# A longer pause, other tile counts and another order of small steps in the side work of an FNet + H3 kernel

## The chip, the cores and the metric

The kernel runs on one core of one Trainium2 chip. The metric is the device time of one execution in microseconds (us), the median of several runs. TensorE is called PE here (its weight loads PEld), VectorE DVE, ScalarE ACT, GpSimd POOL and SyncE SP. SP, ACT and POOL also issue transfers; SPq, ACTq and POOLq mark such an issue.

## What is computed

Four layers on x of 2048 x 576 floats: an FNet layer A, an H3 layer B, and both again with the same weights.

```python
def reference(A_x, A_dft_seq_re, A_dft_seq_im, A_dft_hid_re, A_dft_hid_im, B_q, B_k, B_v, B_shift_k, B_ssm_k, B_ssm_D):
    def _A_ref(x, dft_seq_re, dft_seq_im, dft_hid_re, dft_hid_im):
        a = jnp.einsum("bsd,ed->bse", x, dft_hid_re)
        b = jnp.einsum("bsd,ed->bse", x, dft_hid_im)
        return jnp.einsum("ts,bse->bte", dft_seq_re, a) - jnp.einsum("ts,bse->bte", dft_seq_im, b)
    def _B_ref(q, k, v, shift_k, ssm_k, ssm_D):
        # k_shift: causal convolution of k over 4 rows
        kv = k_shift * v
        # y: causal convolution of kv with ssm_k over all 2048 rows, by FFT of length 4096
        y = y + kv * ssm_D[None, None, :]
        return q * y
    x = A_x
    x = x + _A_ref(_layernorm(x, axis=-1), ...)
    x = x + _B_ref(_layernorm(x, axis=-1), B_k, B_v, ...)
    x = x + _A_ref(_layernorm(x, axis=-1), ...)
    x = x + _B_ref(_layernorm(x, axis=-1), B_k, B_v, ...)
    return x
```

In B only q is the running x. The long convolution of k_shift * v with ssm_k depends on inputs alone, so its result y can be made once, beside the first A, and used by both B layers.

## The kernel before, in words

**Number format.** Every float32 operand of a matmul is split into a rounded part (hi, made by ACT) and a remainder (lo, made by DVE, which subtracts hi), and a product is three matmuls: hi by hi, hi by lo, lo by hi. A split is thus an ACT instruction and then a DVE instruction.

**Main work.** The first A runs in steps n = 0 to 127 (function `layer`): four blocks of rows by real and imaginary part by 16 pieces of the sum. A step has 12 matmuls of 512 columns into four accumulators (`s`) and 2 into a fifth (`rm`). It is handed over in two parts, after 6 matmuls and at its end; at each hand-over the outer loop may put side work in. The constants of a step are loaded by SP (`flts<-in_c_mat`, 256 KB) and split by ACT and DVE (L93, L94) two steps ahead, into three tiles. When a block ends, its second product, over the hidden dimension, is left as eight pieces of 27 matmuls of 288 columns ("hidden pieces", `bk<-w,u`; DVE adds each result on L291). They are put in at odd steps and in the middle of the next block.

**Side work.** The generator `branch` makes y. Its first stage is over before step 47. Then come the two stages that the change edits:

- The **middle stage** has 37 pieces n. Each has a kernel half (`mid_kernel`: three matmuls; ACT evicts the result in three instructions into two `kk` tiles), a signal half (`mid_signal`: three matmuls; DVE multiplies and adds in four instructions, L565 to L568) and, two pieces later, an inverse (`mid_inverse`: three matmuls; ACT evicts into `vo`, ACT's queue issues the store to `vd` in DRAM, L589 and L591). Between the signal half and the inverse, `mid_round` splits the product into the one tile `yf`. `split_mid(n)` splits the input of piece n, and `load_mid(n)` loads it: even ones in one transfer into a `land` tile, odd ones in two, into the `apart` tiles.
- The **inverse stage** has 16 rows j, each in two halves (`i2_products`: six matmuls of 288 columns on `mid`; ACT evicts into a `vo` tile, ACT's queue stores that to `yb`, L650). A row is loaded from `vd` into a `land` tile (`load_row`, SP, 576 KB) and split (`split_row`); its constants come on POOL's queue (`load_fc`). A row load reads what every piece of the middle stage stored, so the first one waits for the last store.

**Order.** All of ACT's side-work instructions go through `act` (L505), which chains each behind the one before in the program's order; `act_split` does the DVE part on L510. Loads go through `load_after` (L167), on SP. SP, ACT, DVE and PE each work through their queues in order; the program's scheduler may put independent work of different stages in another order than the loop does. Three PSUM banks (`bk`) are shared by hidden pieces, the middle stage and the inverse stage.

**Pace.** The outer loop counts main work in `passed` and side work in `spent`. Each `yield` of `branch` names a cost, and at each hand-over up to `GROUPS` = 2 pieces are taken while side work lags:

```python
total = (I2_END + 1 - MID_FROM) * STEP + 3 * 2 * TB * PIECE
work = 37 * sum(MID_COST) + 2 * MID_PAUSE + 32 * I2_COST
...
for _ in range(0 if near else GROUPS):
    if spent < work * min(1.0, passed / total):
        with behind(*added, *evac):
            spent += next(br, work)
```

`total` is 65 x 3.2 + 24 x 3.6 = 294.4 and `work` is 37 x 7.3 + 8 + 32 x 1.9 = 338.9. A pause is a `yield` with a cost and no work.

Of the kernel before, what the change touches and what calls it, by code (L numbers as in the profile page):

```python
# [17 lines left out]
D = 576  # L18
J = S // P
TB = 4  # L20
NT = 512
HD = D // 2
# [19 lines left out]
MW = 504  # L42
MID_COST = (2.9, 2.6, 1.8)
MID_PAUSE = 4.0
BORDER = {J - 1: 0.5, 0: 0.75}
I2_COST = 1.9
GROUPS = 2
# [14 lines left out]
RT_AT = SC_AT + 4 * REM + 5 * WIDE  # L62
# [4 lines left out]
def fnet_h3_kernel(ctx: ExitStack, tc: tile.TileContext, x, c_mat, w_re, w_im, k_pad, v, shift_k,  # L67
# [44 lines left out]
    def flat(words, dt, name):  # L112
        return sb.tile([P, words], dt, tag=name, name=name)
# [17 lines left out]
    def lay(t, at, *sizes):  # L131

        for name, words, n in sizes:
            ring.setdefault(name, Ring()).tiles.extend(t[:, at + i * words:at + (i + 1) * words] for i in range(n))
            at += n * words
        assert at <= t.shape[1], (at, t.shape, sizes)
        return at
# [5 lines left out]
    def two(v):  # L143
        return v.rearrange("p (a n) -> p a n", a=2)
# [11 lines left out]
    flts = flat(FLT, F32, "flts")  # L156
# [8 lines left out]
    def load_after(dst, src):  # L165
        with tc.issue_after(anchor[-1]):
            return nc.sync.dma_start(dst, src).ins  # L167
# [186 lines left out]
    def branch():  # L354
# [148 lines left out]
        def act(*args, **kw):  # L503
            with behind(*last_act[-1:]):
                last_act.append(nc.scalar.activation(*args, **kw).ins)  # L505

        def act_split(h, l, src):
            act(h, src, AF.Copy)
            with behind(*products[-1:]):
                nc.vector.tensor_tensor(l, src, h.bitcast(F32), OP.subtract)  # L510
# [6 lines left out]
        def width(n):  # L517
            first, count = mids[n]
            return MW if n < groups else count * RW

        def load_mid(n):
            if n < len(mids):
                first, count = mids[n]
                w = width(n)
                landed[n] = [r[:, :w] for r in apart] if n % 2 else [ring["land"]()[:, :2 * w]]
                ends = landed[n] if n % 2 else [two(landed[n][0])[:, i] for i in range(2)]
                src = t_d[4 * first:4 * (first + count)]
                if n < groups:
                    src = src.rearrange("q j c s d -> (q j c) s d")[:, :, :MW]
                    if n % 2:  # L530
                        for i in range(2):
                            load_after(ends[i], src[:, i])
                    else:
                        load_after(two(landed[n][0]), src)
                else:
                    src = src.rearrange("(g q) j c s d -> (q j c) s g d", q=4)
                    for i in range(2):
                        load_after(ends[i].rearrange("p (g d) -> p g d", g=count), src[:, i, :, MW:])

        def split_mid(n):  # L540
            if n < len(mids):
                df, at = ring["df"](), 0
                halves[n] = df[:, :2 * width(n)], df[:, 2 * MW:2 * MW + 2 * width(n)]
                for src in landed.pop(n):
                    cs = slice(at, at + src.shape[1])
                    act_split(halves[n][0][:, cs], halves[n][1][:, cs], src)
                    at = cs.stop

        def mid_half(df, o, w):
            ps = bank()  # L550
            mm(ps[:, :w], mc[:, 0, :], df[0][:, o:o + w], True, False)
            mm(ps[:, :w], mc[:, 0, :], df[1][:, o:o + w], False, False)
            mm(ps[:, :w], mc[:, 1, :], df[0][:, o:o + w], False, True)
            return ps[:, :w]

        def mid_kernel(df, w):
            pk, p1, p2 = mid_half(df, w, w), ring["kk"]()[:, :w], ring["kk"]()[:, :w]
            act(p1[lo], pk[lo], AF.Copy)
            act(p1[hi], pk[lo], AF.Copy)
            act(p2[hi], pk[hi], AF.Copy)  # L560
            return p1, p2

        def mid_signal(df, w, p1, p2):
            px = mid_half(df, 0, w)
            nc.vector.tensor_tensor(p1, px, p1, OP.mult)  # L565
            nc.vector.scalar_tensor_tensor(p2[lo], px[hi], -1.0, p2[hi], op0=OP.mult, op1=OP.mult)
            nc.vector.tensor_tensor(p2[hi], px[lo], p2[hi], OP.mult)
            products.append(nc.vector.tensor_tensor(p1, p1, p2, OP.add).ins)  # L568
            return p1

        def mid_round(p1):
            w = p1.shape[1]
            yf = ring["yf"]()
            yf = yf[:, :w], yf[:, w:2 * w]
            act_split(*yf, p1)
            return yf

        def mid_inverse(n, yf):
            w = width(n)
            pv = bank()  # L580
            mm(pv[:, :w], mc[:, 2, :], yf[0], True, False)
            mm(pv[:, :w], mc[:, 2, :], yf[1], False, False)
            mm(pv[:, :w], mc[:, 3, :], yf[0], False, True)
            vo = ring["vo"]()[:, :w]
            act(vo, pv[:, :w], AF.Copy)
            first, count = mids[n]
            dst = v_d[4 * first:4 * (first + count)]
            if n < groups:
                nc.scalar.dma_start(dst.rearrange("q j c d -> (q j c) d")[:, :MW], vo)  # L589
            else:  # L590
                nc.scalar.dma_start(dst.rearrange("(g q) j c d -> (q j c) g d", q=4)[:, :, MW:],  # L591
                                    vo.rearrange("p (g d) -> p g d", g=count))
# [2 lines left out]
        for n in range(2):  # L595
            load_mid(n)
        yield 0
        for n in range(2):
            split_mid(n)
            load_mid(n + 2)  # L600
        for n in range(len(mids)):
            if n > 1:
                mid_inverse(n - 2, yf)
                yield MID_COST[2]
            df, w = halves.pop(n), width(n)
            kk = mid_kernel(df, w)
            if n:
                yf = mid_round(product)
            yield MID_COST[0]
            product = mid_signal(df, w, *kk)  # L610
            split_mid(n + 2)
            load_mid(n + 4)
            yield MID_COST[1]
# [4 lines left out]
        mid_inverse(n, yf)  # L618
        fresh("land", "vo", "df")
        lay(m1, 0, ("df", 4 * D, 2), ("fc", 4 * P, 3))  # L620
        assert lay(flts, 8 + NT, ("land", 2 * D, 3), ("vo", HD, 2)) <= RT_AT - 3 * HD

        def load_row(j):
            if j < J:
                landed[j] = ring["land"]()
                load_after(landed[j], v_d[:, j].rearrange("p c d -> p (c d)"))

        def load_fc(j):
            if j < J:
                fcs[j] = quads(ring["fc"]())  # L630
                load_fr(fcs[j], i2c[j])

        def split_row(j):
            if j < J:
                halves[j] = parts2(ring["df"]())
                act_split(*halves[j], landed.pop(j))
# [4 lines left out]
        def i2_products(hf, j, fc, vf):  # L641
            yo = ring["vo"]()
            ps = bank()
            for c in range(2):
                cs = slice(c * D + hf * HD, c * D + (hf + 1) * HD)
                mm(ps[:, :HD], fc[:, c, :], vf[0][:, cs], c == 0, False)
                mm(ps[:, :HD], fc[:, c, :], vf[1][:, cs], False, False)
                mm(ps[:, :HD], fc[:, 2 + c, :], vf[0][:, cs], False, c == 1)
            act(yo, ps[:, :HD], AF.Copy)
            nc.scalar.dma_start(yb_d[j][:, hf * HD:(hf + 1) * HD], yo)  # L650

        for j in range(3):
            load_fc(j)
        yield MID_PAUSE
        for j in range(3):
            load_row(j)
        yield MID_PAUSE
        for j in range(2):
            split_row(j)
            load_row(j + 3)  # L660
        for j in range(J):
            vf, fc = halves.pop(j), fcs.pop(j)
            i2_products(0, j, fc, vf)
            yield I2_COST
            i2_products(1, j, fc, vf)
            load_fc(j + 3)
            split_row(j + 2)
            load_row(j + 5)
            yield I2_COST

    def sums(src, junk):
# [119 lines left out]
    next(br)  # L791
    spent = passed = 0.0
    total = (I2_END + 1 - MID_FROM) * STEP + 3 * 2 * TB * PIECE
    work = 37 * sum(MID_COST) + 2 * MID_PAUSE + 32 * I2_COST
    for n, whole in layer(get_x0, lambda j: x[:, j, :], done0, pending):
        if (whole or whole is not None and n % J < J - 1) and n <= F1_END:
            at = n if whole else n - 0.5
# [12 lines left out]
        if n >= MID_FROM:  # L810
            if whole is not None:
                passed += STEP * (4 if whole else 3) / 7 * BORDER.get(n % J, 1.05)
            if whole is None or whole and n % 2 == 1 and n % (2 * J) < J - 1 and pending:
# [350 lines left out]
```

## Time and profile before

| | us |
|---|---|
| median of three runs | 1201.93 |
| the three runs | 1203.1, 1197.94, 1201.93 |
| the profiled execution, whole | 1201.85 |
| its span, first to last instruction | 1199.8 |
| PE busy in the span | 1177.4 |
| middle stage, first to last matmul, about | 215 to 530 |
| inverse stage, first to last matmul, about | 541 to 622 |

The page's rows name a line, an engine, an operation and a tile: `ACT L505 ... flts<-bk` is an eviction of a bank by ACT, `mid<-flts` on the same line the rounded part of a split. In brackets behind a row of the timeline stands how long the engine had been idle and what ended that. In a row of windows there follow the busy time of PE, PEld, DVE, ACT and POOL (instructions in parentheses), the granted PE clock as a share of full speed, the busy share of the core's 16 DMA engines, and GB/s. In the waits view the numbers are the total in us, the times, and the longest.

### The profile page before, as it was taken

What the parts mean: (1) busy time and instruction counts of PE and PEld (TensorE: products, weight loads), DVE (VectorE), ACT (ScalarE), POOL (GpSimd) and SP (SyncE); (2) the same over time, 40 slices, a digit from 0 to 9 for tenths busy, and PEclk for the clock granted to TensorE, in tenths of its full rate; (3) what the DMA queues carried; (4) which work ended last, traced back from release to release, by engine and by line L of the source; (5) the groups of instructions that cost most, each with busy time, mean ns of one, the idle gap of its engine ahead of it and who ended that gap; (6) DMA issues with size and microseconds to landing.
All of it is one profiled execution on the core that took longest, in us unless ns stands there. A gap on an engine that the chain in (4) does not pass through costs nothing.

```text
span 1199.8 us, 17259 instructions
## 1 busy us (share of the span) xinstructions
PE 1177.4 (98%) x6077; PEld 1012.8 (84%) x6077; DVE 813.8 (68%) x1335; ACT 615.3 (51%) x1106; POOL 65.8 (5%) x100
## 2 busy tenths in 40 slices
PE   7999999999999999998999999999999999999997
PEld 6888888888888877787888898888888888889997
DVE  7899794677766677643337766774775776874674
ACT  7965665567665566634445667544444445540110
POOL 2200000000000000001001111000000000001111
PEclk9999999999999999999999999999999999999999
DMA  9889897555575546458948687872493497696631
GB/s 356 277 263 321 258 302 240 181 166 174 170 253 182 170 130 171 110 150 271 284 149 281 230 252 235 276 252 88 147 330 93 135 332 269 191 345 191 202 122 40
DMA packets 153768, 257.69 MB, mean 215 GB/s; under 512 B 27601, under 2 KB 68817, under 8 KB 153682
## 3 DMA queue, kind: packets, MB, share of 16 engines
q1 hardware_dynamic: 113074, 205.58, 53.6%
q10 hardware_dynamic: 36000, 42.63, 10.2%
q0 software_dynamic: 4608, 8.39, 2.6%
q8 instruction: 47, 0.77, 0.3%
q14 instruction: 39, 0.32, 0.1%
HBM read 189.89 MB, written 66.65 MB: 214 GB/s over the span
## 4 chain that ended last, share of the span: by engine, by line
PE 89%; DMA 6%; DVE 2%; ACT 1%; issue 1%; SPq 0%; POOLq 0%; POOL 0%; DVEq 0%; ACTq 0%
PE s L76 51%; PE bk L76 33%; PE rm L76 5%; DMA yb<-flts 4%; DMA flts<-in_c_mat 1%; ACT flts L505 1%; DMA vd<-flts 0%; DMA flts<-t 0%; ACT mid L505 0%; DMA flts<-vd 0%; DVE flts L182 0%; DVE u L94 0%; DVE mats L94 0%; DVE mid L510 0%; ACT mats L196 0%
## 5 line engine op out<-in xcount | busy, mean ns | idle before, releaser
L76 PE MATMUL s<-mats 128*128 128x512 f32 x2088 | 524.6, 392 | 0.0
L76 PEld LDWEIGHTS s<-mats 128*128 128x128 f32 x2088 | 386.0, 188 | 80.1 <-DVE mats L94 1.1
L94 DVE TENSOR_TENSOR mats<-flts,mats 128x512 fp32r<-128x512 f32 x201 | 137.6, 688 | 64.6 <-ACT mats L93 59.9
L93 ACT ACTIVATE mats<-flts 128x512 fp32r<-128x512 f32 x201 | 126.0, 628 | 104.2 <-PE bk L76 34.2
L505 ACT ACTIVATE flts<-bk 64x504 f32<-64x504 f32 (+3 forms) x180 | 98.6, 551 | 110.4 <-PE bk L76 76.6
L510 DVE TENSOR_TENSOR mid<-flts,mid 128x1008 fp32r<-128x1008 f32 (+3 forms) x90 | 81.3, 903 | 85.2 <-ACT mid L505 84.9
L76 PE MATMUL bk<-mid 128*128 128x504 f32 (+1 forms) x525 | 122.7, 359 | 5.7 <-ACT mid L505 4.7
L76 PEld LDWEIGHTS bk<-w,u 128*128 128x128 f32 x864 | 118.6, 189 | 8.0 <-ACT flts L505 4.0
L76 PE MATMUL bk<-w,u 128*128 128x288 f32 x864 | 121.9, 297 | 3.1 <-ACT flts L505 2.0
L76 PEld LDWEIGHTS bk<-mid 128*128 128x128 f32 x525 | 87.9, 189 | 25.6 <-ACT mid L505 7.1
L76 PE MATMUL rm<-mats 128*128 128x512 f32 x304 | 95.0, 390 | 0.0
L505 ACT ACTIVATE mid<-flts 128x1008 fp32r<-128x1008 f32 (+3 forms) x90 | 71.2, 799 | 15.1 <-PE bk L76 7.1
L453 ACT ACTIVATE flts<-bk 128x288 f32<-128x288 f32 x128 | 50.7, 410 | 46.9 <-PE bk L76 46.2
L76 PE MATMUL bk<-f1r 128*128 128x288 f32 x384 | 64.3, 300 | 7.2 <-ACT f1r L93 7.0
L76 PEld LDWEIGHTS bk<-f1r 128*128 128x128 f32 x384 | 59.5, 191 | 13.7 <-ACT f1r L93 7.5
L76 PE MATMUL bk<-mats 128*128 128x288 f32 (+1 forms) x376 | 67.8, 317 | 0.0
L76 PEld LDWEIGHTS rm<-mats 128*128 128x128 f32 x304 | 57.0, 188 | 12.2
L76 PE MATMUL s<-t,mats 128*128 128x512 f32 x264 | 64.9, 389 | 0.0
L76 PE MATMUL bk<-mats,t 128*128 128x288 f32 (+1 forms) x368 | 59.3, 303 | 0.0
L76 PEld LDWEIGHTS bk<-mats 128*128 128x128 f32 x376 | 55.6, 188 | 3.4
L185 POOL TENSOR_TENSOR flts<-flts 128x1 f32<-128x1 f32 x35 | 29.7, 848 | 524.3 <-DVE flts L184 524.2
L76 PEld LDWEIGHTS s<-t,mats 128*128 128x128 f32 x264 | 49.6, 188 | 10.3
(149 smaller groups left out, 1404.0 us busy)
## 6 DMA issues: line engine op xcount, KB each, us to landing
flts<-in_c_mat SPq DMA_DIRECT2D x148, 256.0 KB, 3.8
ph<-in_c_mat SPq DMA_DIRECT2D x54, 512.0 KB, 3.8
t<-flts ACTq DMA_DIRECT2D x64, 288.0 KB, 4.5
flts<-in_c_mat SPq DMA_DIRECT2D x30, 512.0 KB, 4.9
flts<-vd SPq DMA_DIRECT2D x16, 576.0 KB, 5.5
vd<-flts ACTq DMA_DIRECT2D x36, 252.0 KB, 3.0
flts<-t SPq DMA_DIRECT2D x16, 504.0 KB, 4.2
ud<-ph ACTq DMA_DIRECT2D x12, 512.0 KB, 5.8
```

The lines of the kernel that those rows point to most:

```text
L76: nc.tensor.matmul(ps, lhsT, rhs, start=first, stop=last, skip_group_check=more)
L93: a = nc.scalar.activation(h, src, AF.Copy).ins
L94: return a, nc.vector.tensor_tensor(l, src, h.bitcast(F32), OP.subtract).ins
L185: pows.append(nc.gpsimd.tensor_tensor(rs, ve, mhalf, OP.pow).ins)
L453: stored[:] = [nc.scalar.activation(so[:, c, :], ps[:, :HD], AF.Copy).ins]
L505: last_act.append(nc.scalar.activation(*args, **kw).ins)
L510: nc.vector.tensor_tensor(l, src, h.bitcast(F32), OP.subtract)
```

## The change

The inverse stage: the pause ahead of its first row's rounding is 9.0 in place of 4.0 (the one ahead of its loads stays 4.0), and `work` grows by 5; two landing tiles in place of three, so two rows are loaded at the start in place of three, and each later load is one row less ahead; six result tiles (`vo`) in place of two, in the same room. The middle stage: `mid_round` of piece n - 1 stands ahead of `mid_kernel` of piece n, so ACT rounds that product before it evicts the kernel half; the split of input 1 and the load of input 3 stand behind the first kernel half, in place of ahead of it.

```diff
+I2_PAUSE = 9.0
...
-        for n in range(2):
-            split_mid(n)
-            load_mid(n + 2)
+        split_mid(0)
+        load_mid(2)
         for n in range(len(mids)):
             if n > 1:
                 mid_inverse(n - 2, yf)
                 yield MID_COST[2]
             df, w = halves.pop(n), width(n)
-            kk = mid_kernel(df, w)
             if n:
                 yf = mid_round(product)
+            kk = mid_kernel(df, w)
+            if not n:
+                split_mid(1)
+                load_mid(3)
             yield MID_COST[0]
             product = mid_signal(df, w, *kk)
             split_mid(n + 2)
...
-        assert lay(flts, 8 + NT, ("land", 2 * D, 3), ("vo", HD, 2)) <= RT_AT - 3 * HD
+        assert lay(flts, 8 + NT, ("land", 2 * D, 2), ("vo", HD, 6)) <= RT_AT - 3 * HD
...
         yield MID_PAUSE
-        for j in range(3):
+        for j in range(2):
             load_row(j)
-        yield MID_PAUSE
+        yield I2_PAUSE
         for j in range(2):
             split_row(j)
-            load_row(j + 3)
+            load_row(j + 2)
         for j in range(J):
...
             split_row(j + 2)
-            load_row(j + 5)
+            load_row(j + 4)
             yield I2_COST
...
-    work = 37 * sum(MID_COST) + 2 * MID_PAUSE + 32 * I2_COST
+    work = 37 * sum(MID_COST) + MID_PAUSE + I2_PAUSE + 32 * I2_COST
```

## The prediction

> **What bounds the kernel now.** The page first: busy shares, then the chain of work that ended last.
>
> ```profile
> PE 1177.4 (98%) x6077; PEld 1012.8 (84%) x6077; DVE 813.8 (68%) x1335; ACT 615.3 (51%) x1106; POOL 65.8 (5%) x100
> PE 89%; DMA 6%; DVE 2%; ACT 1%; issue 1%; SPq 0%; POOLq 0%; POOL 0%; DVEq 0%; ACTq 0%
> ```
>
> PE is the bound; it is idle for 22.4 of 1199.8 us. No matmul is added or removed, so the change can win only idle PE time. The waits view, for PE alone, says where that is:
>
> ```profile
> PE bk L76 <- ACT f1r L93: 7.0, 1, 7.0
> PE bk L76 <- ACT mid L505: 4.7, 4, 3.3
> PE bk L76 <- ACT flts L505: 2.6, 2, 2.0
> PE bk L76 <- DVE flts L291: 1.0, 1, 1.0
> ```
>
> (total us, times, longest.) The 7.0 is the kernel's start, which nothing here touches. The other three rows, 8.3 us in seven waits, are the stages that the change edits.
>
> Idle is not all of the loss: a matmul's row overlaps the next one's.
>
> ```profile
> 628.54 2.72 PE s L76 x12
> L76 PE MATMUL s<-mats 128*128 128x512 f32 x2088 | 524.6, 392 | 0.0
> ```
>
> Starts are 2.72/12 = 0.227 us apart, rows 0.392 long, so an idle of g delays PE by g + 0.16 us. For 288 columns I use 0.132 us between starts (the 27 at 560.54 below: (3.87 - 0.30)/27).
>
> **1. The longer pause ahead of the first inverse row.** The timeline of the entry:
>
> ```profile
> 529.49 0.55 PE L76 MATMUL bk<-mid 128*128 128x288 f32 x3
> 529.88 2.93 PE L76 MATMUL s<-mats 128*128 128x512 f32 x12
> ...
> 530.52 0.37 ACTq L591 DMA_DIRECT2D vd<-flts  x1
> 536.23 1.27 SPq L167 DMA_DIRECT2D flts<-vd  x3
> 536.27 1.75 PE L76 MATMUL s<-mats 128*128 128x512 f32 x7
> 540.12 1.16 ACT L505 ACTIVATE mid<-flts 128x1152 fp32r<-128x1152 f32 x1 [3.25 <-DMA flts<-vd]
> 541.34 0.40 PE L76 MATMUL bk<-mid 128*128 128x288 f32 x1 [3.32 <-ACT mid L505]
> ```
>
> The last middle transform's matmuls start at 529.49, its result is stored at 530.52, the row loads wait for that store until 536.23, row 0 has landed at 540.12, is rounded, and PE goes on at 541.34. This chain takes 11.85 us. PE had 11.85 - 3.48 = 8.37 us of other work to put in it and lost 3.32 + 0.16 = 3.48. Then comes a second loss (PEclk is the third number from the right):
>
> ```profile
> 541.00:543.00 2.00, 1.66 (x11) 1.66 (x12) 1.60 (x2) 1.46 (x2) 0.00 (x0) 0.90 0.95 383
> 543.00:545.00 2.00, 2.00 (x10) 2.00 (x9) 1.11 (x1) 0.41 (x1) 0.00 (x0) 0.50 0.66 124
> 545.00:547.00 2.00, 2.00 (x14) 2.00 (x13) 0.00 (x0) 0.00 (x0) 0.00 (x0) 0.74 0.83 260
> ```
>
> The granted clock falls to half: 2.0 x (0.10 + 0.50 + 0.26) = 1.72 us. The entry costs 5.20 us.
>
> What the edit does follows from the pacing loop. `work` grows from 338.9 to 343.9, `total` stays 294.4. The middle stage's last cost stands at 270.1 in both, so it is reached at 270.1 x 294.4/338.9 = 234.6 us of main work before and 231.2 after; the first inverse row at 278.1 and 283.1 units, 241.6 and 242.4 us. Replaying the loop with its half-step grid, the last transform moves from the first half of step 101 to the first half of step 100; the first row stays in the first half of step 102. So between the two lie, in the loop's order, 28 main matmuls and one hidden-product piece in place of 14 and one: 28 x 0.227 + 27 x 0.132 + 3 x 0.132 = 10.3 us against the chain's 11.85, a wait of 1.5 us. The chip's order is not quite the loop's (before, the loop had 14 main matmuls and a hidden piece there, the trace 35 matmuls, 12 + 2 + 12 + 2 + 7 from 529.88 to the row at 536.27, and no hidden piece: pieces are moved by up to a step and a half). Counted from the trace instead, 8.37 + 14 x 0.227 = 11.55, a wait of 0.3; a row drawn half a step (1.4 us) forward gives some 3.0. I take the middle one, **1.5 left**, bounds 0 and 3.0. Gain 5.20 - 1.5 = **3.7**.
>
> Is the clock loss gone as well? The trace has an idle of 2.00 us (at 560.54, below), and the window around it (rival B) shows 1.00; 3.32 cost 1.72; between them nothing is shown. [...]
>
> **2. Six result tiles.** The groups view of 531 to 626 us, and three rows of the timeline:
>
> ```profile
> L505 ACT ACTIVATE flts<-bk 128x288 f32<-128x288 f32 x32 | 13.1, 410 | 45.4 <-DMA yb<-flts 29.2 <-PE bk L76 16.0 <-issue 0.2
> L505 ACT ACTIVATE mid<-flts 128x1152 fp32r<-128x1152 f32 x16 | 18.6, 1160 | 3.5 <-DMA flts<-vd 3.5
> L510 DVE TENSOR_TENSOR mid<-flts,mid 128x1152 fp32r<-128x1152 f32 x16 | 21.7, 1359 | 44.1 <-ACT mid L505 44.1
> ...
> 560.08 0.41 ACT L505 ACTIVATE flts<-bk 128x288 f32<-128x288 f32 x1 [5.16 <-DMA yb<-flts]
> 560.54 3.87 PE L76 MATMUL bk<-w,u 128*128 128x288 f32 x27 [2.00 <-ACT flts L505]
> 571.21 0.93 PE L76 MATMUL bk<-mid 128*128 128x288 f32 x5 [0.18 <-DVE mid L510]
> 602.77 1.07 PE L76 MATMUL bk<-mid 128*128 128x288 f32 x6 [0.62 <-ACT flts L505]
> ```
>
> With two tiles an eviction waits for the store of the second-last one: 29.2 us of ACT over 16 waits. Three reach PE, through a bank that isn't emptied or a rounding queued behind: 2.16 + 0.34 + 0.78 = 3.28 us. With six tiles a store has five further evictions' time to land, 12 us at 32 in some 80 us; its longest takes 8.3:
>
> ```profile
> DMA to landing us min/median/max: 1.7/3.8/8.3
> flts<-vd SPq DMA_DIRECT2D x16, 576.0 KB, 5.5
> ```
>
> These waits go. What is late next is the rows.
>
> **3. Two landing tiles.** The load of row j+4 waits for the rounding of row j+2; before, that of row j+5 waited for the same rounding, so SP's queue (the constants' loads stand behind it) is held no longer than it was. The lead falls from three rows to two. One tile's round is 5.5 (load) + 1.16 + 1.36 = 8.0 us for two rows; PE takes some 80 us for 16 rows, 10 us for two. It fits, with 2 us to spare for queues. If that cover is gone, ACT waits for a row with evictions and constants behind it. Bounds 0 and 3.0 (a wait like that at 560.54 once, and a small one); I take **0.7**, nearer to the fitting sum. Parts 2 and 3: 3.28 - 0.7 = **2.6**.
>
> **4. Second input split later.** At the start of the middle stage:
>
> ```profile
> 213.76 0.62 ACT L505 ACTIVATE mid<-mid 128x504 fp32r<-128x504 f32 x1 [1.11 <-DMA mid<-t]
> 215.17 0.63 ACT L93 ACTIVATE mats<-flts 128x512 fp32r<-128x512 f32 x1
> 215.84 0.69 DVE L94 TENSOR_TENSOR mats<-flts,mats 128x512 fp32r<-128x512 f32 x1 [2.46 <-ACT mats L93]
> 216.56 0.46 DVE L291 TENSOR_TENSOR flts<-flts,bk 128x288 f32<-128x288 f32 x1
> 217.07 1.46 PE L76 MATMUL bk<-w,u 128*128 128x288 f32 x9 [1.03 <-DVE flts L291]
> ```
>
> ACT stands at input 1's landing, the constant behind it is late, DVE's subtract of it holds the add that empties a bank, and PE loses 1.03 + 0.16 = 1.19. With input 1 split behind the first kernel transform, the constant comes first. Input 3's loads (two, on SP) go out later by the three evictions, 1.8 us; they are needed a whole piece later, some 8 us. Bounds 0 and 1.19; gain **1.0**.
>
> **5. Rounding ahead of the evictions.** Two pieces of the middle stage, and the weight loads' waits of 208 to 531 us:
>
> ```profile
> 339.22 1.78 ACT L505 ACTIVATE flts<-bk 64x504 f32<-64x504 f32 x3 [1.10 <-PE bk L76]
> 339.57 0.69 DVE L568 TENSOR_TENSOR flts<-flts 128x504 f32<-128x504 f32 x1
> 341.05 0.52 PEld L76 LDWEIGHTS bk<-mid 128*128 128x128 f32 x3 [0.45 <-ACT flts L505]
> ...
> 352.73 0.50 PE L76 MATMUL bk<-mid 128*128 128x504 f32 x1 [0.24 <-ACT mid L505]
> 444.30 1.65 PE L76 MATMUL bk<-mid 128*128 128x504 f32 x6 [0.88 <-ACT mid L505]
> ...
> PEld bk L76 <- ACT flts L505: 4.2, 11, 0.5
> ```
>
> Three times PE waits for a rounding that stands behind three evictions (4.7 - 3.3 = 1.4 us, with 3 x 0.16 1.88). It now comes up to 1.8 us sooner: these go. In exchange the evictions stand behind the rounding, and that behind DVE's product of the piece before. At 339.22 the product ends only at 340.26: the evictions would begin at 340.26 + 0.62 = 340.88, 1.66 late, with the signal half's matmul (341.05) and DVE's multiplies behind them. Where the product is ready earlier, the rounding fits into ACT's wait for PE and costs nothing. Eleven weight loads already end a wait on these evictions, so slack there is nil: bounds 0 and 11 x 1.66 = 18.3. I take **1.2**, two roundings of 0.62, as the nearest rows show waits of half a microsecond at most. Net 1.88 - 1.2 = **0.7**.
>
> **Sum.** 3.7 + 2.6 + 1.0 + 0.7 = 8.0. The profiled execution took 1201.85 us, 2.05 beyond its span; the median, 1201.93, is the same. 1201.85 - 8.0 = **1193.9**. Later stages keep PE full, so time won stays won.
>
> **The rivals.** A, the pause hardly helps: the first row is drawn forward on PE as the other pieces are, rest 3.0 plus the clock's 1.72. Gain 0.5 + 2.6 + 1.0 + 0.7 = 4.8: **1197.1**. For it: the order on PE differs from the loop's; against: the transform moves by a whole step.
>
> B, the waits move to the loads:
>
> ```profile
> 540.00:610.00 70.00, 65.77 (x393) 59.13 (x394) 24.93 (x26) 30.01 (x49) 6.89 (x13) 0.98 0.90 277
> 560.00:570.00 10.00, 9.46 (x62) 8.86 (x63) 3.88 (x5) 5.75 (x10) 1.06 (x2) 1.00 0.75 223
> ```
>
> The second number from the right is the DMA engines' share: 0.90 over 70 us, 63 us of transfers. The same bytes in 63 to 65 us would leave nothing; with one tile less of lead, rows come late and take back the 3.28, and the entry's rest is 3.0. Gain 2.2 + 0 + 1.0 + 0.7 = 3.9: **1198.0**. [...]
>
> C, slower: the rounding waits for the product, evictions come late, PE waits at each of the eleven places, 18.3 in place of 1.2: 1193.9 + 17.1 = **1211.0**. It decides from 8.0 + 1.2 = 9.2 us of such waits, 0.84 at each place.
>
> **How the numbers follow.** Forecast 0.60, A 0.14, B 0.16, C 0.10. Runs of before spread by 5 us, so about 0.5%, 6.0 us, is what can be told from no change: the forecast is faster, A and B are the same, C is slower. If all 5.20 + 3.28 + 1.19 + 1.88 = 11.55 us go, 1190.3; the range goes from just below it to above B, 1189.5 to 1200.5, and leaves C out.
>
> **What would show it.** Entry: PE's idle before the first 288-column matmul on `mid` under 2 us, PEclk 1.00 behind it. Results: no ACT wait on `yb`. Landing: ACT's wait on `vd` (3.5 us now) not above some 10 us. Start: no PE wait on L291 near 217. Rounding: no PE wait on `mid` L505 but the entry's; the weight loads' 4.2 us on the evictions not above 6. The prediction is wrong if the waits on evictions or on `vd` grow instead.

## The result, and the profile after

| kernel | median, us | runs | ratio to before, 95% interval | profiled execution (its span) |
|---|---|---|---|---|
| before | 1200.97 | 4, 1197.94 to 1203.1 | 1 | 1201.85 (1199.8) |
| after | 1190.16 | 4, 1189.44 to 1192.66 | 0.9916 [0.9888, 0.9943] | 1190.62 (1188.8) |

The change makes the kernel 10.8 us faster by the medians, 11.2 us by the profiled executions; 8.0 was forecast. The ratios here and below compare means and leave out two disturbed runs, one of p_split (3028.1 us) and one of u_pause4 (1291.8 us), which their medians still count (u_pause4's is 1195.4 us without it). The line numbers of the changed kernel are one higher up to the branch's bodies (L77 is the matmul, L506 `act`, L511 the remainder's subtract).

The page of the changed kernel, busy shares and the chain of work that ended last:

```profile
PE 1172.7 (99%) x6077; PEld 1013.5 (85%) x6077; DVE 814.3 (68%) x1335; ACT 614.6 (52%) x1106; POOL 66.2 (6%) x100
PE 95%; DVE 2%; DMA 1%; ACT 1%; issue 0%; POOL 0%; POOLq 0%; SPq 0%; DVEq 0%; ACTq 0%
```

PE is now idle for 1188.8 - 1172.7 = 16.1 us in place of 22.4, and the transfers' share of the chain fell from 6% to 1%. PE's busy time fell as well, by 4.7 us for the same 6077 matmuls: up to 1.72 us of that is the stretch of half clock at the entry that is gone (the clock is 1.00 from 520 to 600 us). PE's waits, in the view of before (total us, times, longest):

```profile
PE bk L77 <- ACT f1r L94: 6.8, 1, 6.8
PE bk L77 <- ACT flts L506: 0.7, 2, 0.5
PE bk L77 <- ACT flts L454: 0.7, 2, 0.4
PE s L77 <- ACT mats L94: 0.6, 1, 0.6
PE bk L77 <- DVE mid L511: 0.2, 1, 0.2
PE bk L77 <- ACT mid L506: 0.2, 1, 0.2
```

Of the 8.3 us of waits that the change could reach (4.7 on roundings, 2.6 on evictions, 1.0 on the hidden add), 0.9 are left on roundings and evictions and none on the hidden add, and one new wait of 0.6 on a constant came. (L454 is the first stage's eviction, L453 before, where the change edits nothing.) The entry to the inverse rows, timeline (start, duration, engine, line, operation, idle before it):

```profile
521.01 0.56 PE L77 MATMUL bk<-mid 128*128 128x288 f32 x3
...
523.89 0.41 ACT L506 ACTIVATE flts<-bk 128x288 f32<-128x288 f32 x1 [2.29 <-DMA vd<-flts]
...
524.34 0.37 ACTq L592 DMA_DIRECT2D vd<-flts  x1
...
524.59 3.77 PE L77 MATMUL bk<-w,u 128*128 128x288 f32 x27
...
526.65 0.82 SPq L168 DMA_DIRECT2D flts<-vd  x2
...
530.51 1.17 ACT L506 ACTIVATE mid<-flts 128x1152 fp32r<-128x1152 f32 x1 [5.07 <-DMA flts<-vd]
...
531.39 1.52 PE L77 MATMUL s<-mats 128*128 128x512 f32 x6
...
532.75 0.29 PE L77 MATMUL bk<-mid 128*128 128x288 f32 x1
```

No idle stands in front of the row's first matmul at 532.75. Between it and the last transform PE did 34 main matmuls and a hidden piece of 27, 34 x 0.227 + 27 x 0.132 + 3 x 0.132 = 11.7 us, where the kernel before had 35 main matmuls and no piece: there the piece stood ahead of the transform, at 525.89. The row's rounded part was ready at 530.51 + 1.17 = 531.68, 10.7 us after the transform's start: 1.0 us early. That chain was shorter too: the loads were issued 2.3 us behind the store (524.34 to 526.65), 5.7 us before the change (530.52 to 536.23), though the eviction began 2.88 us after the transform's first matmul.

The inverse rows, ACT's groups from 522.5 to 618 us (count, busy and mean ns, idle before and what ended it):

```profile
L506 ACT ACTIVATE mid<-flts 128x1152 fp32r<-128x1152 f32 x16 | 18.6, 1163 | 14.4 <-DMA flts<-vd 14.2
L506 ACT ACTIVATE flts<-bk 128x288 f32<-128x288 f32 x33 | 13.5, 409 | 32.7 <-PE bk L77 30.0 <-DMA vd<-flts 2.3 <-PE rm L77 0.4
```

The 29.2 us on the stores' landing (`yb`) are gone. The evictions now wait for PE, which is as it should be where PE is the bound. ACT's wait on the rows' loads rose from 3.5 to 14.2 us.

**Loss by stage.** The waits leave out the half clock and small stretches, so the loss of every run is also summed here from its matmul records: the distance from one PE matmul's start to the next one's, less 0.227 us (512 or 504 columns) or 0.132 us (288). The stages are divided at 208 us, at the last transform, 6 us behind the first row's first matmul (so that "entry" holds a half clock) and behind the last row. "Rest" is what lies before 208 and after the rows, where the change edits nothing; over all runs it goes from 5.2 to 7.0, which shows how far such a sum wanders by itself.

| kernel | middle | entry | inverse | rest |
|---|---|---|---|---|
| before | 10.9 | 5.2 | 5.3 | 5.2 |
| after | 8.5 | 0.2 | 0.8 | 5.8 |

26.6 less 15.3 is 11.3 us; the two profiled executions differ by 11.2. Each row is a single execution.

### The profile page after: what moved, and what is told of

It reads as the page before. It is cut to its first block, busy times and chain, and to the rows that moved or that the text cites. A ratio compares the mean times of both kernels' runs of the same rounds, so it can differ in the third digit from the quotient of the medians.

```text
span 1188.8 us, 17284 instructions
## 1 busy us (share of the span) xinstructions
PE 1172.7 (99%) x6077; PEld 1013.5 (85%) x6077; DVE 814.3 (68%) x1335; ACT 614.6 (52%) x1106; POOL 66.2 (6%) x100
## 3 DMA queue, kind: packets, MB, share of 16 engines
q10 hardware_dynamic: 36000, 42.63, 10.3%
## 4 chain that ended last, share of the span: by engine, by line
PE 95%; DVE 2%; DMA 1%; ACT 1%; issue 0%; POOL 0%; POOLq 0%; SPq 0%; DVEq 0%; ACTq 0%
PE s L77 54%; PE bk L77 35%; PE rm L77 6%; DMA flts<-in_c_mat 1%; ACT flts L506 0%; DMA flts<-in_ssm_k 0%; DVE flts L183 0%; DVE u L95 0%; ACT mid L506 0%; DVE mats L95 0%; DVE mats L200 0%; ACT mats L197 0%; ACT u L94 0%; DVE mid L511 0%; POOL flts L186 0%
## 5 line engine op out<-in xcount | busy, mean ns | idle before, releaser
L77 PE MATMUL s<-mats 128*128 128x512 f32 x2088 | 524.1, 392 | 0.8 <-ACT mats L94 0.6
L77 PEld LDWEIGHTS s<-mats 128*128 128x128 f32 x2088 | 386.8, 188 | 79.8 <-DVE u L95 1.5
L506 ACT ACTIVATE flts<-bk 64x504 f32<-64x504 f32 (+3 forms) x180 | 99.0, 550 | 82.9 <-PE bk L77 76.4
L77 PEld LDWEIGHTS bk<-w,u 128*128 128x128 f32 x864 | 117.8, 188 | 4.7 <-ACT flts L506 1.3
L77 PE MATMUL bk<-w,u 128*128 128x288 f32 x864 | 120.5, 295 | 0.5 <-ACT flts L506 0.5
L77 PE MATMUL bk<-mid 128*128 128x504 f32 (+1 forms) x525 | 120.1, 356 | 0.7 <-ACT flts L506 0.2
L511 DVE TENSOR_TENSOR mid<-flts,mid 128x1008 fp32r<-128x1008 f32 (+3 forms) x90 | 80.3, 902 | 45.6 <-ACT mid L506 45.5
L77 PEld LDWEIGHTS bk<-mid 128*128 128x128 f32 x525 | 88.0, 188 | 16.7 <-ACT flts L506 1.8
L77 PE MATMUL rm<-mats 128*128 128x512 f32 x304 | 94.5, 390 | 0.0
L506 ACT ACTIVATE mid<-flts 128x1008 fp32r<-128x1008 f32 (+3 forms) x90 | 71.9, 799 | 37.2 <-DMA flts<-vd 14.2
L454 ACT ACTIVATE flts<-bk 128x288 f32<-128x288 f32 x128 | 50.7, 410 | 48.8 <-PE bk L77 48.3
L77 PE MATMUL bk<-f1r 128*128 128x288 f32 x384 | 64.7, 301 | 7.4 <-ACT f1r L94 6.8
L77 PEld LDWEIGHTS bk<-f1r 128*128 128x128 f32 x384 | 59.9, 192 | 13.9 <-ACT f1r L94 6.8
L77 PE MATMUL bk<-mats 128*128 128x288 f32 (+1 forms) x376 | 67.8, 317 | 0.0
L77 PEld LDWEIGHTS rm<-mats 128*128 128x128 f32 x304 | 57.0, 188 | 12.3
L77 PE MATMUL s<-t,mats 128*128 128x512 f32 x264 | 64.9, 389 | 0.0
L292 DVE TENSOR_TENSOR flts<-flts,bk 128x288 f32<-128x288 f32 x48 | 21.8, 453 | 61.5 <-PE bk L77 61.3
L77 PE MATMUL bk<-mats,t 128*128 128x288 f32 (+1 forms) x368 | 59.3, 303 | 0.0
L77 PEld LDWEIGHTS bk<-mats 128*128 128x128 f32 x376 | 55.5, 188 | 3.4
```

The lines of the kernel that those rows point to most:

```text
L77: nc.tensor.matmul(ps, lhsT, rhs, start=first, stop=last, skip_group_check=more)
L292: added[:] = [nc.vector.tensor_tensor(rows[hf], rows[hf], ps[:, :HD], OP.add).ins]
L454: stored[:] = [nc.scalar.activation(so[:, c, :], ps[:, :HD], AF.Copy).ins]
```

## The experiments

All were timed against the kernel before in five rounds. The first eight shared two sets of its runs (medians 1201.96 and 1200.89), the last four one (1201.38); medians of different sets are compared by their ratios. The table lists all by what they hold of the change: P the pause, T the tile counts, R the rounding ahead of the evictions, S the later split.

| label | holds | median, us | ratio, 95% interval | middle | entry | inverse | rest |
|---|---|---|---|---|---|---|---|
| p_pause | P | 1202.57 | 0.9998 [0.9986, 1.0011] | 12.7 | 0.5 | 6.4 | 6.8 |
| p_tiles | T | 1197.12 | 0.9957 [0.9944, 0.9970] | 10.7 | 2.9 | 4.5 | 6.3 |
| p_round | R | 1201.16 | 0.9989 [0.9974, 1.0005] | 8.9 | 4.9 | 5.4 | 5.4 |
| p_split | S | 1202.20 | 1.0011 [0.9995, 1.0028] | 10.3 | 4.7 | 5.8 | 6.5 |
| u_pause4 | T R S | 1196.04 | 0.9950 [0.9933, 0.9967] | 7.3 | 4.6 | 0.7 | 6.8 |
| u_pause6 | T R S, pause 6.5 | 1195.18 | 0.9955 [0.9937, 0.9973] | 6.9 | 4.9 | 0.9 | 6.0 |
| u_two_results | all, two result tiles | 1191.04 | 0.9922 [0.9903, 0.9942] | 8.4 | 0.6 | 2.4 | 5.4 |
| u_round_late9 | all, R from piece 9 on | 1191.48 | 0.9919 [0.9901, 0.9937] | 9.7 | 0.1 | 0.8 | 6.2 |
| x_tiles_round | T R | 1196.68 | 0.9962 [0.9950, 0.9974] | 7.6 | 5.9 | 0.8 | 7.0 |
| x_tiles_split | T S | 1198.10 | 0.9979 [0.9966, 0.9992] | 10.5 | 6.0 | 5.4 | 6.4 |
| x_tiles_pause | P T | 1194.94 | 0.9951 [0.9939, 0.9964] | 12.8 | 0.6 | 0.8 | 5.8 |
| x_no_split | P T R | 1189.19 | 0.9904 [0.9891, 0.9917] | 7.5 | 0.3 | 0.8 | 5.4 |

The stages are those of one profiled execution. For p_tiles and x_tiles_split it was the slowest of their runs (1199.09 and 1203.08), so their stages add up to more loss than their medians have, 2 and 5 us.

### The four parts, each alone

p_pause, on the kernel before:

```diff
+I2_PAUSE = 9.0
...
             load_row(j)
-        yield MID_PAUSE
+        yield I2_PAUSE
...
-    work = 37 * sum(MID_COST) + 2 * MID_PAUSE + 32 * I2_COST
+    work = 37 * sum(MID_COST) + MID_PAUSE + I2_PAUSE + 32 * I2_COST
```

> Before, with the longer pause alone (9.0 in place of 4.0, and work with it; three landing tiles, two result tiles). Theory (each edit takes its own PE wait away, and they add up): the entry's idle of 3.3 us and its half clock are gone, 5 us less, so about 1196 against 1201; the eviction waits on yb stay, one of about 2 us reaching PE. Rival 1 (the inverse stage's eviction waits only reach PE because its first rows come late): they go as well, 8 to 9 us less, about 1192. Rival 2 (the early rounding is what brings the last transform forward): the entry keeps 2 us or more of idle, under 3 us less, 1198 or above.

None of the three expectations holds whole. Alone the pause is worth nothing (0.9998), yet the entry's loss fell from 5.2 to 0.5. The same time came back elsewhere: 1.8 us in the middle stage, 1.1 in the rows and 1.6 in the rest. The pacing loop spends the 5 units of the pause on nothing and takes the other side work earlier; the 1.6 of the rest is within what the rest wanders by itself. The rows of this kernel, timeline:

```profile
602.83 0.41 ACT L506 ACTIVATE flts<-bk 128x288 f32<-128x288 f32 x1 [1.89 <-DMA yb<-flts]
603.27 0.33 ACTq L651 DMA_DIRECT2D yb<-flts  x1
603.29 0.83 PEld L77 LDWEIGHTS bk<-mid 128*128 128x128 f32 x6 [2.23 <-ACT flts L506]
603.30 0.93 PE L77 MATMUL bk<-mid 128*128 128x288 f32 x5 [1.80 <-ACT flts L506]
```

With two result tiles an eviction still stands behind a store, and PE behind the eviction.

p_tiles:

```diff
-        assert lay(flts, 8 + NT, ("land", 2 * D, 3), ("vo", HD, 2)) <= RT_AT - 3 * HD
+        assert lay(flts, 8 + NT, ("land", 2 * D, 2), ("vo", HD, 6)) <= RT_AT - 3 * HD
...
-        for j in range(3):
+        for j in range(2):
             load_row(j)
...
-            load_row(j + 3)
+            load_row(j + 2)
...
-            load_row(j + 5)
+            load_row(j + 4)
```

> Before, with six result tiles and two landing tiles alone (pauses 4.0 and 4.0). Theory: no ACT wait on yb, the inverse stage after its entry loses under 1 us in place of 5.3, the entry keeps its 3.3 us of idle and its half clock: 3.3 to 4.7 us less, about 1197. Rival (two landing tiles give rows that come late): ACT's wait on vd is above 15 us and part of it reaches PE, under 2 us less, 1199 or above.

It is worth 0.43%, 5 us, the largest of the four: the time is the theory's, but ACT's waits are the rival's. The profiled execution doesn't show clean rows: their loss only went from 5.3 to 4.5. It was the slowest, just 2.8 us faster than that of before, so where the other 2 us of the median come from is in no kept trace. ACT's wait on the loads and SP's longest from 531 to 624 us, and one place of the timeline:

```profile
ACT mid L505 <- DMA flts<-vd: 28.1, 12, 4.6
...
SPq L283 <- DMA xa<-flts: 18.8, 4, 7.3
```

```profile
571.17 0.33 SPq L283 DMA_DIRECT2D flts<-in_x  x1
...
571.61 0.88 SPq L167 DMA_DIRECT2D flts<-vd  x2
...
576.12 1.17 ACT L505 ACTIVATE mid<-flts 128x1152 fp32r<-128x1152 f32 x1 [3.90 <-DMA flts<-vd]
...
577.71 0.39 ACT L505 ACTIVATE flts<-bk 128x288 f32<-128x288 f32 x1
...
578.56 0.41 ACT L505 ACTIVATE flts<-bk 128x288 f32<-128x288 f32 x1 [0.46 <-ACT flts L505]
...
579.75 1.43 PE L76 MATMUL bk<-mid 128*128 128x288 f32 x9 [1.29 <-ACT flts L505]
```

ACT stands for 3.90 us at a row that hasn't landed, two evictions stand behind that rounding in ACT's order, and PE waits for the banks. This is rival B's mechanism: the 29.2 us on `yb` became 28.1 us on `vd`. The load itself was not slow (571.61 to 576.12, 4.5 us), and its tile had been free since 565.85, when row 6's remainder was made. It went out late: in SP's order a load of `in_x` (L283) stands ahead of it, and that one stood 7.3 us, until 571.17, for the landing of an `xa` store that SP had issued at 563.42. The rest of this execution's gain was the entry: PE was idle for 2.6 us there, and no half clock followed (1.00 from 538 to 546), where 2.1 us in p_round were followed by one (last section).

p_round and p_split:

```diff
             df, w = halves.pop(n), width(n)
-            kk = mid_kernel(df, w)
             if n:
                 yf = mid_round(product)
+            kk = mid_kernel(df, w)
```

> Before, with the rounding ahead of the next evictions alone. Theory: no PE wait on a rounding of the middle stage, and the eleven half-microsecond waits on evictions become fewer; new waits where the product is late: 1 to 2 us less, about 1199.5. Rival (evictions come late behind the product): the waits on evictions grow, no gain or a loss, 1201 or above.

```diff
-        for n in range(2):
-            split_mid(n)
-            load_mid(n + 2)
+        split_mid(0)
+        load_mid(2)
...
+            if not n:
+                split_mid(1)
+                load_mid(3)
             yield MID_COST[0]
```

> Before, with the second input's split behind the first kernel half alone. Theory: the PE wait of 1.0 us on DVE L291 near 217 us is gone or down to 0.3, 0.5 to 1 us less, about 1200.3, hardly to be told from before by the time alone. Rival (the entry of the middle stage is bound by the loads anyway): the wait is there a piece later, no gain.

Neither can be told from the kernel before. p_round took 2.0 us out of the middle stage, where it acts, but the profiled execution had a half clock twice, at the entry and in the rows (granted clock 0.996 over the span, 0.50 from 561 to 563). p_split took the wait near 217 away, as its theory has it (loss from 208 to 222 us: 1.3 before, 0.6 here), but changed none of the three stages by more than 0.6 us.

The four alone add up to about 5 + 1 + 0 - 1 = 5 us; together they give 10.8. The next question was which of them need each other.

### Taken out of the changed kernel

u_pause4 sets the pause back to 4.0; u_pause6 has 6.5 in the same line.

```diff
-I2_PAUSE = 9.0
+I2_PAUSE = 4.0
```

> After, with the pause of 4.0 again (work 338.9). Theory: the entry's idle comes back, 2 to 3.5 us, and with over 3 us the half clock: 1193 to 1195. Rival 2 (the early rounding and the later split alone shorten the chain): idle under 1 us, within 1 us of after.

> After, with a pause of 6.5 (work 341.4), half way. Theory: the last transform comes half a step earlier than before, so 0 to 2 us of idle are left, full clock: 1190 to 1192. If it leaves 2 to 3.3 us of idle, the granted clock tells whether such an idle costs it.

Both give back 4 to 5 us by the ratios. The entry loses 4.6 and 4.9 in place of 0.2, the middle stage 1.2 and 1.6 less than with the pause of 9.0. Half of the longer pause does as little as none of it, and u_pause6's expectation (half a step, at most 2 us of idle) is missed. The timeline of u_pause6:

```profile
526.09 0.55 PE L77 MATMUL bk<-mid 128*128 128x288 f32 x3
...
527.12 0.37 ACTq L592 DMA_DIRECT2D vd<-flts  x1
...
532.53 0.80 SPq L168 DMA_DIRECT2D flts<-vd  x2
...
532.87 1.75 PE L77 MATMUL s<-mats 128*128 128x512 f32 x7
...
537.64 0.45 PE L77 MATMUL bk<-mid 128*128 128x288 f32 x1 [3.02 <-ACT mid L506]
```

The transform still has 8.4 us of PE work behind it, and the row comes 11.55 us after it: the order is that of before. The order on PE can be counted in every trace, as the main matmuls ahead of the last transform and ahead of the first row:

| kernels | ahead of the transform | ahead of the row | hidden piece between |
|---|---|---|---|
| the six with the pause of 9.0 | 1386 | 1420 | yes |
| the other eight, u_pause6 among them | 1400 | 1435 | no |

There are two orders and none between them. The pause alone picks one, in every mix with the other edits that was run, and somewhere between 6.5 and 9.0 it jumps by a whole step of 14.

u_two_results and u_round_late9:

```diff
-        assert lay(flts, 8 + NT, ("land", 2 * D, 2), ("vo", HD, 6)) <= RT_AT - 3 * HD
+        assert lay(flts, 8 + NT, ("land", 2 * D, 2), ("vo", HD, 2)) <= RT_AT - 3 * HD
```

> After, with two result tiles in place of six (two landing tiles, everything else as after). Theory: evictions wait on yb again, some 25 us of ACT, and 3 to 5 us of it reach PE: 1193 to 1195 against 1190. Rival 1 (with rows in time these waits do not reach PE): within 1 us of after.

```diff
-            if n:
+            if n > 8:
                 yf = mid_round(product)
             kk = mid_kernel(df, w)
+            if 0 < n <= 8:
+                yf = mid_round(product)
```

> After, with the rounding behind the evictions again in the first eight pieces, where pieces stand densest. Theory (the 2.4 us that PE loses between 262 and 269 us come from evictions behind a rounding that waits for DVE's product): they go, 1 to 2 us less than after, 1188 to 1189. Rival (these losses are the density itself, three banks and DVE's queue): same as after, or PE waits on the rounding again.

With two result tiles in the changed kernel ACT waits as long as it ever did (519 to 618 us):

```profile
ACT flts L506 <- DMA yb<-flts: 30.8, 13, 4.3
...
ACT mid L506 <- DMA flts<-vd: 6.1, 2, 5.1
```

Yet the rows lose only 2.4 us, 1.6 more than in the changed kernel, and the medians are 0.9 us apart, inside the intervals. Rival 1 holds: 30 us of ACT's waiting hardly reached PE in this order of the work. u_round_late9 was to see whether the rounding's new place causes the losses that the changed kernel has at 266 to 269 us (next section). They went, but one longer wait of PE on a rounding took their place:

```profile
PE bk L77 <- ACT mid L506: 2.4, 2, 2.2
```

A half clock followed it (0.61 and 0.53 in the windows of 267 to 269 and 269 to 271 us), and the middle stage lost 9.7 in place of 8.5 us: the expectation's rival. What this place needs is the pause: from 255 to 272 us PE loses 2.6 us in the changed kernel and 2.3 in x_tiles_pause (below), which has the old order of the rounding, but 0.2 in u_pause4.

### Pairs and triples

The rows are clean (0.7 to 0.9) in every kernel with T R S, and not with T alone. Four kernels built from the hunks above, on the kernel before, were to find what T needs, and what P needs.

> Kernel before with the tiles (six result, two landing) and the rounding ahead of the evictions; the old pause and the old split. The tiles alone left 4.3 us of PE loss in the inverse rows (ACT waited 28.1 us on vd), the same tiles with rounding, split and a pause of 4 left 0.7. Theory R (the rounding cleans the rows): inverse loss about 1 us, middle loss down to 7, entry 3 to 5: 1193.5 to 1195.5. Theory S (the split does it, as it sends the second input's loads later on SP): inverse loss stays at 4, 1196 to 1198. Theory T (neither by itself; the tiles' late rows are an accident of one order, and any other edit of the order takes them away): clean here and with the split too, both 1194 to 1196.

The rows are clean as theory R has it, but the time is 1.2 us above its range and no better than that of the tiles alone (0.9962 beside 0.9957). The profiled entry cost 5.9, with 6.8 us of half clock (0.81, 0.50, 0.50 and 0.50 in the four windows of 2 us from 537 to 545); that doesn't explain the median, for a run with a granted clock of 0.999 took 1196.31 all the same.

> Kernel before with the tiles and the later split; the old pause and the old order of the rounding. Theory R: inverse loss stays at about 4 us, start loss down by 0.5: 1196 to 1198. Theory S: inverse loss about 1 us: 1194 to 1196. Theory T: clean as well, 1194 to 1196.

Theories S and T fall: the rows lose 5.4 us. 1.7 of it is a half clock (0.59 and 0.56 in the two windows of 2 us from 598 to 602). The timeline shows the mechanism of p_tiles once more; here SP stood 6.8 us, until 587.01, at the `in_x` load, and the row's load behind it took 6.9:

```profile
594.37 1.17 ACT L505 ACTIVATE mid<-flts 128x1152 fp32r<-128x1152 f32 x1 [6.45 <-DMA flts<-vd]
...
598.00 2.42 PE L76 MATMUL bk<-mid 128*128 128x288 f32 x10 [2.78 <-ACT flts L505]
```

> Kernel before with the tiles and the pause of 9; no change to the rounding and the split. If the pause needs only the tiles (they take away what it had moved into the inverse rows): entry 0, inverse 1 to 2, the middle as in the pause alone (11.8): 1192 to 1193.5. If it needs the rounding too, the rows stay late as with the tiles alone: entry 0, inverse 4, middle 11 to 12: 1195 to 1197.

Rows and entry are clean, so the tiles with the pause alone do that; the middle stage loses 12.8 (p_pause has 12.7 in the table, where the expectation says 11.8), and with it the time (1194.94) falls between the two theories. ACT's wait on the loads is half of that in p_tiles (527 to 622 us, 5.0 of it at the entry):

```profile
ACT mid L506 <- DMA flts<-vd: 14.1, 7, 5.0
```

> The changed kernel with the second input split where it was before, so pause, tiles and rounding. By the prediction's term for the split (1.0 us at the start of the middle stage) 1191.0 to 1191.5, with PE waiting about 1 us on the hidden add near 217 again. If the split is worth nothing, as alone: 1190.0 to 1190.6. If the split is what cleans the inverse rows: inverse loss 3 to 5, 1193 to 1195.

Without the later split the kernel is no slower: 0.9904 [0.9891, 0.9917] beside 0.9916 [0.9888, 0.9943]. This is the lowest time of all, 1189.19, though the intervals overlap. PE's waits over the whole kernel, all of them:

```profile
PE bk L77 <- ACT f1r L94: 6.8, 1, 6.8
PE s L77 <- ACT mats L94: 0.6, 1, 0.6
PE s L77 <- DVE u L95: 0.3, 1, 0.3
PE bk L77 <- ACT flts L454: 0.2, 1, 0.2
```

No wait on the hidden add (L292 here) is among them, with the second split in its old place.

**What follows.** By the ratios the tiles alone give 5 us. The rounding added to them gives -0.6 and the pause 0.7, both inside the intervals, but the two together 6.4 (x_no_split); S adds nothing. So *the pause and the rounding need each other*: this the times show, beside the tiles. The traces show where. With the tiles and the rounding, the pause takes the entry from 5.9 (3.4 of it the half clock of that execution) to 0.3; with the tiles and the pause, the rounding takes the middle stage from 12.8 to 7.5. Without the rounding the pause raised the middle's loss by 2.1 (beside the tiles) and 1.8 (alone), with it by -0.1 (x_tiles_round to x_no_split) and 1.2 (u_pause4 to the changed kernel). That the closer pace of the middle stage leaves a late rounding less room is the likely reason; it is argued, not shown. The pause with the rounding and the old tiles was not run.

In the profiled executions the tiles' rows are late alone and with the split, and clean with the rounding or the pause. Since x_tiles_round is no faster than p_tiles, whose profiled execution was its slowest, the times don't confirm that this is a property of the kernel and not of the execution. SP's longest wait on an `xa` store goes with it: 7.3 and 6.8 us where rows were late, 6.1 in x_tiles_round, 4.9 in x_tiles_pause, 5.8 in the changed kernel. Why it differs is not settled. Such a wait costs PE only where the slack is gone: 3.90 us of ACT at a load cost PE 1.29 in p_tiles, and in x_tiles_round, whose row of waits on the loads follows (527 to 622 us), no wait behind the entry's reached PE.

```profile
ACT mid L505 <- DMA flts<-vd: 17.0, 10, 3.6
```

## Why the prediction was right, and where its steps were not

**The bound and the sum.** PE's idle was the place to look, and the ceiling of 11.55 us (1190.3) that closed the range is where the time went: 1190.16. The forecast of 8.0 fell short since its three deductions, 1.5 at the entry, 0.7 for late rows and 1.2 for roundings, were too dear or paid for by other gains. That a sum of four terms came so near is in part luck: it took the edits as independent, and alone they give 5 us. The clock has a share that no term names: span times what the granted clock lacks is 3.8 us in the mean of the 63 runs of before that stood beside the experiments and 1.5 in the 4 of after.

**Entry, 3.7 forecast.** The transform went ahead by a whole step, as the replay had it, and the whole loss of 5.2 went, the half clock with it. The term that was mis-sized is the rest of 1.5: it took 10.3 us of work against a chain of 11.85; the trace has 11.7 against 10.7. Two things behind it came out otherwise. The first row did not stay in its place: it too was drawn forward, by 15 main matmuls, which is rival A's condition. So 34 main matmuls lie between, one less than before. What filled the gap is the hidden piece, which now stands behind the transform: 27 x 0.132 = 3.6 us, where the replay, which had a piece there before as well, counted 14 more main matmuls, 3.2 us. That these are alike is luck. And the loads followed the store 3.4 us sooner, which had not been foreseen. What the step did not see is that a pause is no gift: it closes up the rest of the side work (p_pause: +1.8 in the middle), which was counted nowhere. Rival B's gain of 2.2 here counts a rest of 3.0 us as free of a half clock, which no run shows: behind idles of 3.0 us in x_tiles_round and x_tiles_split 3.38 and 2.84 us of clock were lost (last section).

**Results and landing, 2.6 forecast.** The `yb` waits went as forecast, and the rows' loss fell by 4.5 us, 3.3 of it at the three waits that the prediction listed as 3.28. The reasons came out differently. Six result tiles are not most of what makes the rows clean: with two, the changed kernel loses 1.6 us more in them. And the two landing tiles did not fit "with 2 us to spare for queues": in p_tiles the round from row 6's rounding (563.29) to row 8's (576.12) took 12.8 us against 10, for SP's queue alone took 5.8 of it, and rival B came true there. SP's queue was to be held no longer than before; its longest wait on an `xa` store was 5.6 us before and 7.3 in p_tiles. The loads themselves took about as long as before: the median is 5.5 us before, 5.8 in p_tiles and 5.1 after. In the changed kernel even the 0.7 was too dear.

**Split, 1.0 forecast.** Right for the wait, wrong for the time. The wait near 217 goes by the split alone (p_split), though the time doesn't show it, and a new loss of 0.4 stands at the next piece, near 221.6, as its rival had it. In the set the split has nothing to take away: without it x_no_split loses 0.25 us there. The step took a wait in one order of the work as belonging to the edit nearest to it; the same wait moves with the pause.

**Rounding, 0.7 forecast.** Mis-sized, and for the whole kernel the largest error. The three waits of 1.88 went (0.2 left), the weight loads' waits on the evictions fell from 4.2 to 3.0 us over six in place of eleven, though the longest rose from 0.5 to 0.9, and rival C did not come. The price that the step expected can be seen at one place of the changed kernel's timeline:

```profile
264.57 0.62 ACT L506 ACTIVATE mid<-flts 128x504 fp32r<-128x504 f32 x1
...
265.08 1.78 ACT L506 ACTIVATE flts<-bk 64x504 f32<-64x504 f32 x3
...
266.91 0.95 PE L77 MATMUL bk<-mid 128*128 128x504 f32 x3 [0.24 <-ACT flts L506]
...
268.50 0.73 PE L77 MATMUL s<-mats 128*128 128x512 f32 x2 [0.64 <-ACT mats L94]
```

Here PE waits for evictions behind a rounding, and then for a constant that ACT reaches late: 1.7 us of loss from 265.9 to 268.5. It is near the 1.2 that was taken, but not the rounding's alone, since u_pause4, with the same rounding and the old pause, doesn't have it. The gain is larger than 1.88: 2.0 us of the middle stage by itself, 3.1 beside the tiles, 5.3 beside tiles and pause (12.8 to 7.5). So the edit seems to take away what the pause would bring, and a sum over parts has no place for that.

**The marks.** Entry without idle, no ACT wait on `yb`, no L291/L292 wait of PE, the weight loads below 6: as written. One PE wait of 0.2 on a rounding of the middle stage is left where none was to be. ACT's wait on `vd` passed the mark of 10 us (14.2, of which 5.07 is the entry's chain itself), and by the prediction's last sentence its growth was a sign of being wrong. PE has no wait at all in the rows, so the mark was set on the wrong quantity.

## What to carry to other kernels

Where edits share one in-order engine and one pacing loop, their worth alone is not their worth together: here 5 us alone, 10.8 in the set, two of the four that pay only together, and one (the split) that could be left out. Count the work that is to cover a chain from the trace's own rows, and look for the jumps in which a schedule moves, for half of a longer pause may do nothing. A load's round has the time in its issuing queue as well as its own duration: here 5.8 us behind another load that waited. And a long wait on an engine that isn't the bound (30 us of ACT on its stores) is a price only where a row of the bound engine names it.

## What the hardware showed that was not expected

The half clock does not go by the length of PE's idle alone. Windows of p_round (length, busy PE, PEld, DVE, ACT, POOL with counts, granted clock, DMA share, GB/s), after an idle of 2.1 us that ended near 558.6:

```profile
557.00:559.00 2.00, 0.40 (x3) 0.40 (x4) 0.00 (x0) 0.86 (x2) 0.00 (x0) 1.00 0.56 184
559.00:561.00 2.00, 2.00 (x14) 2.00 (x13) 1.36 (x2) 2.00 (x5) 0.00 (x0) 0.73 0.35 116
561.00:563.00 2.00, 2.00 (x10) 2.00 (x9) 1.76 (x2) 0.80 (x1) 0.00 (x0) 0.50 0.76 188
```

and of p_tiles, after a longer one that ended at 541.13:

```profile
538.00:540.00 2.00, 0.48 (x3) 0.06 (x1) 0.07 (x1) 0.08 (x1) 0.00 (x0) 1.00 0.97 387
540.00:542.00 2.00, 0.87 (x6) 0.87 (x7) 0.89 (x1) 1.73 (x2) 0.00 (x0) 1.00 0.98 384
542.00:544.00 2.00, 2.00 (x17) 2.00 (x16) 1.83 (x2) 0.93 (x2) 0.00 (x0) 1.00 0.39 51
```

2.1 us cost a half clock, 2.6 us cost none. Eight idles of 2 us and more, with the granted clock around each and what it lost (length of a window times what its clock lacks, summed):

| run | PE's idle, us | granted clock, windows of 2 us | clock lost, us |
|---|---|---|---|
| before, to 541.34 | 3.32 | 0.90, 0.50, 0.74 (541 to 547) | 1.72 |
| before, to 560.54 | 2.00 | 1.00 (558 to 564) | 0 |
| p_round, to near 558.6 | 2.1 | 1.00, 0.73, 0.50, 0.92 (557 to 565) | 1.70 |
| p_tiles, to 541.13 | 2.6 | 1.00 (538 to 546) | 0 |
| u_round_late9, to near 267 | 2.2 | 1.00, 0.61, 0.53 (265 to 271) | 1.72 |
| x_tiles_round, entry | 3.0 | 0.81, 0.50, 0.50, 0.50 (537 to 545) | 3.38 |
| x_tiles_split, entry | 3.0 | 0.58, 0.50, 0.50 (540 to 546) | 2.84 |
| x_tiles_split, to 598.00 | 2.78 | 0.59, 0.56, 1.00 (598 to 604) | 1.70 |

In x_tiles_round and at the entry of x_tiles_split the last window still has 0.50, so the loss may go on behind it. What decides whether an idle of 2.0 to 2.6 us is followed by a half clock these windows do not show, and no kernel was made to try it. For reading a result it means that, of four such idles here, two cost no clock (2.00 and 2.6 us) and two 1.70 and 1.72 us (2.1 and 2.2), so up to 1.7 us of the difference between two profiled executions can be the clock's and not the waits'.
